# Attention outputs moved to a bank of the feed-forward pool, and first-layer matrices converted 1024 columns at a time

## The chip, the cores and the metric

One core of one Trainium2 chip runs the whole program. The metric is the device time of one execution in microseconds (us); lower is better. Engines: PE (TensorE matmul), DVE (VectorE), ACT (ScalarE), POOL (GpSimd), SP (the queue that issues all DMAs here). PSUM, the accumulator memory that PE writes, has eight banks of 512 float32 columns on 128 partitions.

## The reference

Top-k attention, then two feed-forward blocks, in float32 (weights arrive as float64):

```python
# q, k, v: (4 batches, 8 heads, 576, 64)
scores = scale * q @ k.T
kth = np.partition(scores, -32, axis=-1)[..., -32:-31]     # the 32nd largest of a row
scores = np.where(scores >= kth, scores, -1e9)
attn = softmax(scores); x = attn @ v                       # -> (2304 tokens, 512)
h = x @ w_in;  y = np.maximum(0.01 * h, h) @ w_out         # 512 -> 2048 -> 512
h = np.maximum(np.maximum(y @ w1, y @ w2), y @ w3)         # 512 -> 768, three products
out = h @ moe2_w_out                                       # 768 -> 512
```

## The kernel before, in words

**Attention.** The 2304 tokens are cut into 20 blocks (128 tokens, or 64 at the end of a batch). A *step* handles two heads of a 128-token block or four heads of a 64-token block: 72 steps, 18 for each batch, numbered 0 to 71 in the order of `steps`; the last six make the last 192 tokens. In `attention(i)` PE makes the scores of a head (line 718) into the tile `s`, ACT copies them to SBUF as `S` (L723), DVE finds the 32 largest by four rounds of MAX8 and three of MATCH_REPLACE8 (L738, L740), ACT exponentiates (L788), DVE and POOL mask (L793, L797, L800), ACT and POOL split the result into two float16 parts (L802, L804), one DMA transposes them into `pt` (L807), PE multiplies with v (L833 to L835) into the tile `av`, whose 65th column per head is the row's sum. DVE reads those sums and inverts them (L840, L842), ACT scales the outputs into `xs` (L844), and `xhl` is transposed by DMA into `xu` (L870), the input of the feed-forward part.

**Feed-forward.** `ffn(u)` handles ten units of 192, 128, seven times 256, and 192 tokens. A matmul in float32 accuracy is three float16 matmuls (`three`, L876 to L878). A unit has 16 first-layer tiles of 4 such triples (`h_tile`, drained by ACT at L924), 16 x 4 second-layer triples into the accumulators `acc` (`y_acc`, drained at L974), then 18 x 4 triples of the second block's three products (`m_tile`; ACT drains the first product at L1017, DVE takes the maximum with the other two at L1021) and 6 x 4 output triples (`o_acc`, drained at L1049). Units 0 to 4 need all steps up to 5, 9, 17, 25 and 33; unit 9 needs step 71.

**Weights.** `prep_w` converts the float64 matrices with three DVE operations of integers per piece of `CW` = 512 columns (L499, L502, L505), by way of a PSUM tile: kinds "i" and "o" (w_in and w_out, eight chunks of 1024 columns for either) through one of the two `acc` banks per piece, kinds "t" and "z" (the second block) through a bank of the `h` pool.

**PSUM.** Eight banks: two for one tensor `sav`, in which the scores `s` take columns 0 to 287 of each bank and the attention outputs `av` columns 288 to 417; two `acc` tiles; a pool `h` of four. The pool is shared by the first-layer tiles (at most 2 at a time, `hH`), the tiles of the second block (3, `hM`), conversion pieces (1, `hW`) and small sums over partitions (no limit of their own). The framework that places semaphores serialises accesses of different engines to one bank of one tensor, so whatever touches `s` and whatever touches `av` wait for each other.

**Order.** `Plan.run` is a list scheduler in the program's builder: with estimated durations, latencies and buffer counts (`NB`) it fixes the order of instructions on each engine. Of an engine's ready instructions the one that can start first goes next, and among equals the one of smaller priority number (L139 to L156). An engine then runs its list in that order and waits where something isn't ready. The planner treats `s` and `av` as independent buffers. `RLAG` is an extra delay that it adds before the read of the sums (L840):

```python
279    sav = ps.tile([P, 2, 512], F32, name="sav")
280    ZONE["s"] = [sav[:, :, :288]]
281    ZONE["av"] = [sav[:, :, 288:418]]
...
465    CW = 512
...
680    RLAG = 3.0
```

Of the kernel before, what the change touches and what calls it, by code (L numbers as in the profile page):

```python
# [9 lines left out]
F32 = mybir.dt.float32  # L10
# [19 lines left out]
P = 128  # L30
# [176 lines left out]
def dve(n, fast=False):  # L207
    return (n / (2 if fast else 1) / 0.96 + 69) / 1000
# [6 lines left out]
def dma(nbytes):  # L215
    return nbytes / 255e3
# [3 lines left out]
def attention_moe_kernel(ctx, tc, qk, v, w_in, w_out, w123, w2o, outT):  # L220
# [8 lines left out]

    NB = {"xu": 2, "raw": 2, "hl": 1, "k2": 7, "kt": 4, "qt": 2, "vt": 4, "S": 3, "w": 1, "m": 2, "nb": 2, "pp": 1,  # L230
          "phl": 1, "pt": 1, "r": 2, "xs": 1, "xhl": 1, "f16t": 4, "yj": 1,
          "s": 1, "av": 1, "acc": 2, "h": 4, "junk": 1, "xcap": 2, "pr": 8, "ph": 4, "ra": 3, "fi": 6, "ft": 9, "rw": 3, "fz": 3, "rc": 2, "hH": 2, "hM": 3, "hW": 1, "kH": 2, "kM": 5, "fH": 2, "fM": 2}
    PSUM_TAGS = ("s", "av", "acc", "h")
    plan = Plan(NB, {"raw", "av", "junk", "hl", "k2", "h", "f16t", "rc"})
    op = plan.op
# [2 lines left out]
    def buf(tag, shape, dt=F32):  # L238
        pl = ps if tag in PSUM_TAGS else sb

        def make():
            cnt[0] += 1
            if tag in ZONE:
                return ZONE[tag].pop(0)
            return pl.tile(shape, dt, tag=tag, bufs=NB[tag], name=f"{tag}_{cnt[0]}")

        b = plan.buf(tag, make)
        if tag in ZONE:
            b.done = lambda: ZONE[tag].append(b.ap)
        return b  # L250

    def fbuf(tag, ph, shape, dt=F32):
        b = buf(tag, shape, dt)
        b.also = (plan.buf({"h": "h", "k2": "k", "f16t": "f"}[tag] + ph, lambda: 1),)
        return b
# [20 lines left out]
            "ph": [wof[:, 11264 + 1152 * i:12416 + 1152 * i].rearrange("p (a s) -> p a s", a=2) for i in range(4)],  # L276
            "fz": [w2f[:, 1536 * e:1536 * e + 1536].bitcast(I32) for e in range(1, 4)]}
    NCOL = 318
    sav = ps.tile([P, 2, 512], F32, name="sav")
    ZONE["s"] = [sav[:, :, :288]]  # L280
    ZONE["av"] = [sav[:, :, 288:418]]
    colt = cp.tile([P, NCOL], F32, name="colt")
    cpos = [0]

# [176 lines left out]

    SC = {}
    ZT = "xu"
    CVK = "iotz"
    CW = 512
    CVX = 0.0
    PRW0 = -13.5
    GATES = {1: [], 2: [("d", 0, 0, 0, 1)]}

    def prep_w(kind, c, parts, hi, lo, colnorm, n2c, s, bi, pr, tags, guard=((), (), []), gate=()):  # L470
# [8 lines left out]
        for i, saps in enumerate(parts):  # L479
            nf = sum(n for _, n in saps)  # L480
            f = buf(tags[1], [P, 768 if tags[1] in ("raw", "xu") else 512], I32)
            o = 0
            for sap, n in saps:
                raw = buf(tags[0], [P, 768])
                op(SP, 0.55, lambda raw=raw, sap=sap, n=n: Y.dma_start(raw().bitcast(I64)[:, :n], sap),
                   w=([(f, "ld")] if tags[1] in ("raw", "xu", "k2") or tags[0] in ("raw", "xu") else []) + [raw, (key, "ld")],
                   r=list(gate) + zr + (zf + [("l1", hp, a) for hp in range(HP) for a in range(2)] * (kind == "z" and ZT == "raw") + guard[2] * (tags[1] in ("raw", "xu")) if kind in "tz" else []), pr=PRW0 if (kind, c) == ("i", 0) else pr,
                   dma=dma(P * n * 8))
                for q in range(0, n, CW):
                    cw = min(CW, n - q)  # L490
                    w = lambda raw=raw, q=q, cw=cw: raw().bitcast(I32)[:, 2 * q:2 * (q + cw)].rearrange("p (n t) -> p n t", t=2)
                    t = lambda f=f, cw=cw, q=q + o: f()[:, q:q + cw]
                    pb = None
                    if kind in CVK:
                        pb = buf("acc", [P, 2, UN]) if kind in "io" else fbuf("h", "W", [P, 512])
                    m = t if pb is None else (lambda pb=pb, cw=cw, two=kind in "io": (
                        pb().rearrange("p a n -> p (a n)") if two else pb()).bitcast(I32)[:, :cw])
                    mk_ = [(f, o)] if pb is None else [pb]
                    op(DVE, dve(cw, pb is None) + CVX * (pb is not None), lambda w=w, m=m: V.tensor_scalar(  # L499
                        m(), w()[:, :, 1], 3, 0x3FFFFFFF, op0=ALU.logical_shift_left, op1=ALU.bitwise_and),  # L500
                       r=[raw] + zr + zf, w=mk_, pr=pr)
                    op(DVE, dve(cw) + CVX * (pb is not None), lambda w=w, m=m: V.scalar_tensor_tensor(  # L502
                        m(), w()[:, :, 0], 29, m(), op0=ALU.logical_shift_right, op1=ALU.bitwise_or),
                       r=[raw] + zr + zf, w=mk_, pr=pr)
                    op(DVE, dve(cw) + CVX * (pb is not None), lambda w=w, t=t, m=m: V.scalar_tensor_tensor(  # L505
                        t(), w()[:, :, 1], -0x40000000, m(), op0=ALU.bitwise_and, op1=ALU.bitwise_or),
                       r=[raw] + zr + zf + mk_ * (pb is not None), w=[(f, o)], pr=pr)
                for q in range(0, n, 512):
                    m = min(n - q, 512)
                    sq.append(((f, o), lambda f=f, q=q + o, m=m: f()[:, q:q + m].bitcast(F32), m))  # L510
                o += n
            fs.append((f, [(f, x) for x in np.cumsum([0] + [n for _, n in saps[:-1]]).tolist()],
                       lambda f=f, n=nf: f()[:, :n].bitcast(F32), nf))
# [68 lines left out]
    def w1_prep(f, pr):  # L582
        prep_w("t", f, [[(w123[f, j], 512)] for j in range(3)],
               [w1[:, f, 0, j] for j in range(3)], [w1[:, f, 1, j] for j in range(3)],
               (P, lambda i, kk: (i, kk == 0, kk == 3)), c1(ct, f), c1(s_t, f), c1(bt, f), pr,
               ("rw", "ft" if 1 <= f < 4 else "k2"),
               (["ZA", "ZB"] if f == 0 else [], ["ZR"] if f == 0 else [("ZF", f - 2)] if f >= 3 else [],
                ["ZR"] if f < 3 else [("ZF", f - 2)]), gate=GATES[2])

    def w2_prep(e, pr):  # L590
        for hp in range(HP) if ZT == "raw" else ():
# [85 lines left out]
        return TE + TS * i if i < NE else TA0 + TA * i  # L677

    EXPP = 4
    RLAG = 3.0  # L680
    COLD = 1.7
    NCOLD = 8
    FM = 1
# [12 lines left out]
    def attention(i):  # L696
# [115 lines left out]
            XHL[blk] = buf("xhl", [P, 2, HP, P], F16)  # L812
        xhl = XHL[blk]
        xs = buf("xs", [P, 4, 64])
        avb = buf("av", [P, 512])
        av = lambda: avb().rearrange("p x (h e) -> p x h e", e=65)
        avh = lambda a: av()[:, a // 2, a % 2] if not full else av()[:, 0, a]
        for j in range(2):
            vt = VT[b, hps[j]]

            def avm(j=j, vt=vt):
                hs = [(j, slice(0, P), j)] if full else [(hh, slice(64 * hh, 64 * hh + 64), 2 * j + hh)
                                                        for hh in range(2)]
                for hh, qs, a in hs:
                    o = avh(a)[:qs.stop - qs.start, :]
                    for c in range(5):
                        if c < 4:
                            ch, k = c + 5 * j, 2 * c + hh
                        else:
# [7 lines left out]
            op(PE, 15 * mm(64) * (1 if full else 2) * (COLD if i < NCOLD else 1), avm, r=[pt] + [(vt, x) for x in range(3)], w=[avb, (xs, "a"), (xhl, "a", i)], pr=pa)  # L837
        nh = 2 if full else 4
        r = buf("r", [P, 8])
        op(DVE, 0.07, lambda: V.tensor_scalar(r()[:n, 0:nh].rearrange("p (x h) -> p x h", h=2),  # L840
                                             av()[:n, 0:nh // 2, :, 64], 1e-9 * PS, None, op0=ALU.add), r=[avb], w=[(r, 0)], pr=pr, lag=RLAG)
        op(DVE, 0.08, lambda: V.reciprocal(r()[:n, 4:4 + nh], r()[:n, 0:nh]), r=[(r, 0)], w=[(r, 1)], pr=pr)  # L842
        for h in range(nh):
            op(ACT, act(64, True, 1), lambda h=h: A.activation(xs()[:n, h], avh(h)[:n, 0:64], AF.Copy,  # L844
# [35 lines left out]
    def accs(n):  # L880

        if n <= P:
            a = [buf("acc", [P, 4, P])] * 4
            return (lambda e: a[e]()[:, e, :n]), (lambda e: (a[e], e)), (lambda e: (a[e], "st")), (0,)
        a = [buf("acc", [P, 2, UN]) for _ in range(2)]
        return ((lambda e: a[e // 2]()[:, e % 2, :n]), (lambda e: (a[e // 2], e)), (lambda e: (a[e // 2], "st")),
                (0, 2))

    MAXP = 40
# [304 lines left out]
```

## Time and profile before

| | |
|---|---|
| median of 3 runs | 1131.72 us (1130.45 to 1133.53) |
| the profiled execution's own time | 1129.44 us |
| its span, first to last instruction | 1127.3 us |
| mean granted TensorE clock | 0.958 of full |
| busy: PE / DVE / ACT / POOL | 917.1 / 972.9 / 757.2 / 687.1 us (81 / 86 / 67 / 61%) |

The span is what the trace covers; the time outside it is 2.1 us. A busy share is an average over stretches with different limits: DVE has little to do before the first scores and after the last step, PE has little before the weights are ready. A line such as `L840` is the line of the kernel that issued the instruction; `r<-sav` reads "writes r, reads sav".

### The profile page before, as it was taken

How to read it: one execution, taken by the hardware profiler on the slowest of the kernel's cores; microseconds unless marked ns; L12 is line 12 of the kernel's file. 1: busy time of each engine (PE TensorE's matmuls, PEld its weight loads, DVE VectorE, ACT ScalarE, POOL GpSimd, SP SyncE). 2: the span in 40 equal slices, each digit the busy share in tenths (PEclk: the TensorE clock that was granted, in tenths of full speed). 3: DMA queues.
4: the chain of work that ended last, by engine and by line, in shares of the span. 5: the costliest groups of instructions: out<-in, count | busy, mean ns of one | idle time of the engine just before them, and what ended most of it. 6: DMA issues, size and time to landing. Idle time of an engine off the chain costs nothing.

```text
span 1127.3 us, 27415 instructions
## 1 busy us (share of the span) xinstructions
PE 917.1 (81%) x10292; PEld 800.9 (71%) x10292; DVE 972.9 (86%) x2154; ACT 757.2 (67%) x1625; POOL 687.1 (61%) x1054
## 2 busy tenths in 40 slices
PE   2253236764798998998879899989999998999998
PEld 1132235753698887987768788878888887888998
DVE  3999999999899999999999899899999999995101
ACT  7578757987468666568778665685886665665342
POOL 5475657776458655568678555675887566466121
PEclk9999996875799999999999999999999999999999
DMA  8748457667334432335664423363663433432000
GB/s 297 232 120 258 150 148 211 161 177 150 81 77 103 83 87 52 82 69 143 165 164 97 82 64 72 62 157 75 153 155 77 103 62 53 79 66 53 24 1 16
DMA packets 268517, 125.79 MB, mean 112 GB/s; under 512 B 237408, under 2 KB 255328, under 8 KB 266336
## 3 DMA queue, kind: packets, MB, share of 16 engines
q1 hardware_dynamic: 268384, 124.04, 45.1%
q8 instruction: 81, 1.33, 0.5%
q14 instruction: 52, 0.43, 0.1%
HBM read 62.65 MB, written 14.16 MB: 68 GB/s over the span
## 4 chain that ended last, share of the span: by engine, by line
PE 47%; DVE 16%; ACT 11%; DMA 10%; POOL 7%; issue 6%; SPq 1%; POOLq 0%; ACTq 0%; DVEq 0%
PE h L876 8%; PE h L877 8%; PE h L878 8%; DMA pt<-phl 6%; PE acc L877 5%; PE acc L876 5%; PE acc L878 5%; PE sav L718 4%; DVE m L738 4%; DVE w L740 3%; ACT S L723 2%; PE sav L833 2%; PE sav L834 2%; PE sav L835 2%; DVE w L505 2%
## 5 line engine op out<-in xcount | busy, mean ns | idle before, releaser
L738 DVE MAX8 m<-w 128x8 f32<-128x576 f32 x432 | 309.8, 746 | 0.2 <-DVE r L840 0.2
L937 POOL TENSOR_TENSOR f16t<-k,f16t 128x256 f16<-128x256 f32 (+2 forms) x220 | 144.4, 658 | 175.5 <-ACT f16t L931 150.2
L804 POOL TENSOR_TENSOR phl<-pp,phl 128x576 f16<-128x576 f32 x144 | 184.1, 1288 | 50.5 <-ACT phl L802 49.8
L740 DVE MATCH_REPLACE8 w<-m,w 128x576 f32<-128x576 f32 x288 | 212.0, 741 | 0.0
L876 PE MATMUL h<-k,w 128*128 128x256 f16 (+2 forms) x720 | 187.2, 264 | 7.3 <-ACT k L977 4.0
L877 PE MATMUL h<-k,w 128*128 128x256 f16 (+2 forms) x720 | 187.0, 264 | 3.4 <-POOL k L979 3.3
L878 PE MATMUL h<-k,w 128*128 128x256 f16 (+2 forms) x720 | 186.9, 264 | 0.0
L877 PE MATMUL acc<-f16t,wo 128*128 128x256 f16 (+2 forms) x640 | 167.0, 265 | 5.3 <-POOL f16t L937 5.0
L876 PE MATMUL acc<-f16t,wo 128*128 128x256 f16 (+2 forms) x640 | 166.9, 265 | 0.9 <-ACT k L974 0.5
L878 PE MATMUL acc<-f16t,wo 128*128 128x256 f16 (+2 forms) x640 | 166.9, 265 | 0.0
L718 PE MATMUL sav<-kt,qt 128*128 128x288 f16 (+5 forms) x800 | 109.7, 288 | 61.9 <-ACT S L723 45.9
L876 PE MATMUL h<-xu,wi 128*128 128x256 f16 (+1 forms) x576 | 154.9, 269 | 6.1 <-DMA xu<-xhl 5.3
L877 PE MATMUL h<-xu,wi 128*128 128x256 f16 (+1 forms) x576 | 154.9, 269 | 0.0
L878 PE MATMUL h<-xu,wi 128*128 128x256 f16 (+1 forms) x576 | 154.9, 269 | 0.0
L802 ACT ACTIVATE phl<-pp 128x576 f16<-128x576 f32 x144 | 96.8, 679 | 54.4 <-DVE pp L793 22.7
L788 ACT ACTIVATE pp<-S,nb,colt 128x576 f32<-128x576 f32 x144 | 121.2, 860 | 16.9 <-POOL phl L804 9.3
L718 PEld LDWEIGHTS <-qt 128*128 128x128 f16 (+1 forms) x800 | 64.7, 109 | 87.3 <-issue 71.7
L931 ACT ACTIVATE f16t<-k 128x256 f16<-128x256 f32 (+2 forms) x220 | 85.7, 392 | 52.3 <-DVE k L1021 49.6
L800 POOL TENSOR_TENSOR pp<-pp,S 128x576 f32<-128x576 f32 x72 | 92.1, 1279 | 43.4 <-DVE S L797 32.7
L833 PE MATMUL sav<-vt,pt 128*128 128x65 f16 (+1 forms) x800 | 92.7, 203 | 29.3 <-DMA pt<-phl 22.8
L924 ACT ACTIVATE k<-h,colt 128x256 f32<-128x256 f32 (+2 forms) x160 | 71.0, 451 | 64.1 <-PE h L878 63.8
L723 ACT ACTIVATE S<-sav 128x576 f32<-128x576 f32 x144 | 92.4, 642 | 29.6 <-PE sav L718 14.5
(136 smaller groups left out, 2643.3 us busy)
## 6 DMA issues: line engine op xcount, KB each, us to landing
w<-in_w SPq DMA_DIRECT2D x18, 512.0 KB, 3.9
w<-in_w_in SPq DMA_DIRECT2D x8, 1024.0 KB, 7.2
w<-in_w_out SPq DMA_DIRECT2D x8, 1024.0 KB, 5.0
raw<-in_qk SPq DMA_DIRECT2D x24, 288.0 KB, 3.4
dqk<-hl SPq DMA_DIRECT2D x48, 144.0 KB, 2.5
kt<-dqk SPq DMA_DIRECT2D x16, 288.0 KB, 3.3
qt<-dqk SPq DMA_DIRECT2D x144, 32.0 KB, 2.2
raw<-in_v SPq DMA_DIRECT2D x12, 352.0 KB, 3.4
```

The source lines that it names most:

```text
L718: T.matmul(p()[osl, h, o:o + w], q()[:, hh, st, :n], k()[:, hh, kc:kc + w], start=st == 0, stop=st == 1, skip_group_check=True)
L723: op(ACT, act(S, True), lambda t=t, p=p: A.activation(t().rearrange("p (a s) -> p a s", a=2), p()[:, :, :288], AF.Copy), r=[p], w=[(Sp, j) ...
L738: op(DVE, dve(S) * 1.03, lambda mc=mc, src=src: V.max(mc(), src()), r=rd, w=[(m, j, 0, r)], pr=pd)
L740: op(DVE, dve(S) * 1.03 + 0.06, lambda mc=mc, src=src, j=j: V.match_replace(out=wj(j), in_to_replace=mc(), in_values=src(), imm_value=NEG) ...
L788: op(ACT, act(S, aps=2), lambda j=j, es=es: A.activation(pp()[:, j], Sb[j](), AF.Exp, bias=nb()[:, j:j + 1], scale=es[:, 0:1]), r=[(Sp, j) ...
L802: op(ACT, act(S), lambda j=j: A.activation(phl()[:, 0, j], pp()[:, j], AF.Copy), r=[(pp, j)], w=[(phl, 0, j)], pr=pr)
L804: op(POOL, pool(S), lambda j=j: G.tensor_tensor(phl()[:, 1, j], pp()[:, j], phl()[:, 0, j], op=ALU.subtract), r=[(pp, j), (phl, 0, j)], w= ...
L833: T.matmul(o, hc, vh, start=c == 0, stop=False, skip_group_check=True)
L876: T.matmul(out, wt(0), xt(0), start=first, stop=False, skip_group_check=True)
L877: T.matmul(out, wt(0), xt(1), start=False, stop=False, skip_group_check=True)
L878: T.matmul(out, wt(1), xt(0), start=False, stop=last, skip_group_check=True)
L937: op(POOL, pool(N) + 0.044, lambda: G.tensor_tensor(hl()[:, 1, :N], g()[:, 0, :N], hl()[:, 0, :N], op=ALU.subtract), r=[(g, 0), (hl, 0)], ...
```

## The change

The attention outputs of a step go to a bank of the `h` pool, at most one at a time (`hA`), and all heads of a step lie in that one bank; the scores `s` keep two banks as a tensor of their own. The two `acc` banks become one tensor `acct`, so that kinds "i" and "o" are converted 1024 columns at a time through both banks. Kinds "t" and "z" keep 512. `RLAG` becomes 2.0. The loads of the second block's first matrices (`w1_prep`) are gated on another DMA of batch 0. The constants `CVK`, `CW`, `CVX` go; their values made no difference to the planned durations of the other kinds.

```diff
-          "s": 1, "av": 1, "acc": 2, "h": 4, ... "hH": 2, "hM": 3, "hW": 1, ...
+          "s": 1, "av": 1, "acc": 2, "h": 4, ... "hH": 2, "hM": 3, "hW": 1, "hA": 1, ...
-    sav = ps.tile([P, 2, 512], F32, name="sav")
-    ZONE["s"] = [sav[:, :, :288]]
-    ZONE["av"] = [sav[:, :, 288:418]]
+    acct = ps.tile([P, 2, 512], F32, name="acct")
+    ZONE["acc"] = [acct[:, x] for x in range(2)]
+    accw = acct.rearrange("p a n -> p (a n)").bitcast(I32)
...
+                CW = 1024 if kind in "io" else 512
                 for q in range(0, n, CW):
...
-                    if kind in CVK:
-                        pb = buf("acc", [P, 2, UN]) if kind in "io" else fbuf("h", "W", [P, 512])
+                    if kind in "io":
+                        mk_ = [buf("acc", [P, 512]) for _ in range(2)]
+                        m = lambda cw=cw: accw[:, :cw]
+                    else:
+                        pb = fbuf("h", "W", [P, 512])
+                        mk_ = [pb]
+                        m = lambda pb=pb, cw=cw: pb().bitcast(I32)[:, :cw]
...
-                ["ZR"] if f < 3 else [("ZF", f - 2)]), gate=GATES[2])
+                ["ZR"] if f < 3 else [("ZF", f - 2)]), gate=[("d", 0, 1, 0, 1)])
...
-    RLAG = 3.0
+    RLAG = 2.0
...
-        avb = buf("av", [P, 512])
-        av = lambda: avb().rearrange("p x (h e) -> p x h e", e=65)
-        avh = lambda a: av()[:, a // 2, a % 2] if not full else av()[:, 0, a]
+        avb = fbuf("h", "A", [P, 512])
+        av = lambda: avb()[:, :260].rearrange("p (h e) -> p h e", e=65)
+        avh = lambda a: av()[:, a]
...
-        op(DVE, 0.07, lambda: V.tensor_scalar(r()[:n, 0:nh].rearrange("p (x h) -> p x h", h=2),
-                                             av()[:n, 0:nh // 2, :, 64], 1e-9 * PS, None, op0=ALU.add), r=[avb], w=[(r, 0)], pr=pr, lag=RLAG)
+        op(DVE, 0.07, lambda: V.tensor_scalar(r()[:n, 0:nh], av()[:n, 0:nh, 64], 1e-9 * PS, None, op0=ALU.add), r=[avb], w=[(r, 0)], pr=pr, lag=RLAG)
...
-        a = [buf("acc", [P, 2, UN]) for _ in range(2)]
+        a = [buf("acc", [P, 512]) for _ in range(2)]
```

## Rows read from the trace of the kernel before

**Rows 1.** Busy time by stage: stretch, length, busy of each engine, PEclk, DMA share, GB/s.
```profile
0.00:184.00 184.00, 67.00 (x579) 46.78 (x580) 162.50 (x351) 130.11 (x215) 106.24 (x182) 0.95 0.66 200
184.00:378.00 194.00, 147.62 (x1918) 134.35 (x1917) 182.95 (x414) 143.90 (x330) 131.32 (x212) 0.83 0.56 132
378.00:582.00 204.00, 185.15 (x2023) 160.64 (x2022) 193.12 (x433) 141.75 (x310) 133.92 (x197) 1.00 0.44 104
582.00:1127.00 545.00, 517.28 (x5776) 459.15 (x5775) 434.32 (x959) 341.45 (x771) 315.64 (x466) 0.99 0.36 77
```

**Rows 2.** PE's timeline where unit 4 starts.
```profile
582.24 0.37 PE L876 MATMUL h<-xu,wi 128*128 128x256 f16 x1 [5.34 <-DMA xu<-xhl]
```

**Rows 3.** Waits of DVE over the whole span: us in total, times, longest.
```profile
DVE r L840 <- PE sav L718: 15.0, 14, 2.7
DVE r L840 <- ACT S L723: 7.0, 8, 2.2
DVE r L840 <- PE sav L835: 3.2, 1, 3.2
```

**Rows 4.** The timeline around one late read of the sums: start, us, engine, line.
```profile
639.74 0.19 PE L835 MATMUL sav<-vt,pt 128*128 128x65 f16 x1
...
640.09 0.74 DVE L738 MAX8 m<-w 128x8 f32<-128x576 f32 x1
...
642.72 0.66 PE L718 MATMUL sav<-kt,qt 128*128 128x64 f16 x6
...
643.48 0.16 DVE L840 TENSOR_SCALAR r<-sav 128x2 f32<-128x2 f32 x1 [2.65 <-PE sav L718]
...
645.78 0.31 ACT L844 ACTIVATE xs<-sav,r 128x64 f32<-128x64 f32 x1 [0.74 <-PE sav L718]
```

**Rows 5.** Waits of PE, 582 to 1127 us: us in total, times, longest.
```profile
PE sav L833 <- DMA pt<-phl: 8.0, 8, 2.7
...
PE sav L718 <- ACT S L723: 2.5, 5, 1.5
PE sav L718 <- ACT xs L844: 2.3, 4, 1.4
...
PE sav L833 <- ACT S L723: 1.6, 2, 0.8
...
PE sav L718 <- DVE r L840: 1.0, 1, 1.0
```

**Rows 6.** Waits of DVE, 0 to 378 us.
```profile
DVE r L840 <- PE sav L718: 3.9, 3, 1.7
```

**Rows 7.** Waits of DVE, 378 to 582 us.
```profile
DVE r L840 <- PE sav L718: 4.4, 4, 1.6
...
DVE r L840 <- ACT S L723: 1.5, 1, 1.5
```

**Rows 8.** DVE's timeline inside the conversion of w_out.
```profile
111.29 0.69 DVE L502 SCALAR_TENSOR_TENSOR acc<-w,acc 128x512 int32<-128x512 int32 x1
...
112.01 0.69 DVE L505 SCALAR_TENSOR_TENSOR w<-w,acc 128x512 int32<-128x512 int32 x1
...
121.68 1.27 DVE L499 TENSOR_SCALAR acc<-w 128x512 int32<-128x512 int32 x2
122.87 1.28 DVE L502 SCALAR_TENSOR_TENSOR acc<-w,acc 128x512 int32<-128x512 int32 x2
```

**Rows 9.** Conversion on DVE, groups by shape: count, busy us, mean ns.
```profile
L499 DVE TENSOR_SCALAR h<-w 128x512 int32<-128x512 int32 x18 | 12.2, 678 | 0.6 <-DMA w<-in_w 0.6
L499 DVE TENSOR_SCALAR h<-xu 128x384 int32<-128x384 int32 x8 | 4.4, 554 | 1.9 <-DMA xu<-in_w2o 1.9
```

**Rows 10.** Line 499 for w_in and w_out: duration ns min/median/max, first and last start.
```profile
L499 DVE TENSOR_SCALAR acc<-w x32: 678/682/695, 9.7 to 134.3; 128x512 int32<-128x512 int32 x32
```

**Rows 11.** Issues of line 384, batch 0: ns min/median/max, first and last start.
```profile
L384 SPq DMA_DIRECT2D dqk<-wo x16: 574/592/687, 11.3 to 31.0; - x16
```

**Rows 12.** Issues of line 485, w1 to w3, the same columns.
```profile
L485 SPq DMA_DIRECT2D w<-in_w x18: 327/402/601, 147.7 to 215.5; - x18
```

## What the change does to the time, predicted before it was run

> **What bounds the kernel now.** I read the busy time by stage first, with cuts where unit 0 begins on PE, and units 2 and 4 (184, 378 and 582 us) [rows 1]. Up to 378 us DVE is the full engine: 162.5 of 184 and 183.0 of 194 us, while PE has 67.0 and 147.6. From 378 to 582 us both are nearly full, DVE 193.1 and PE 185.2 of 204 us, and what starts unit 4 is its tokens: PE sat idle 5.34 us for the transposed outputs of step 33 [rows 2]. From 582 us to the end PE has 517.3 of 545 us, 95%, and DVE only 434.3: there the end is set by PE's work, and only a PE wait that goes makes the program shorter. So before 582 us a saving on DVE counts, and after it a saving on PE.
>
> Then the waits of DVE: the read of the sums, L840, waited 15.0 us for score matmuls (L718), 7.0 us for the copy of scores (L723), and only once, 3.2 us, for the matmuls whose result it reads (L835) [rows 3]. The timeline shows one case [rows 4]. The last attention matmul ends at 639.93, DVE is free at 640.83, yet L840 runs at 643.48, behind the next score matmuls, which write the same banks. It cost DVE 2.65 us, and the second read of the outputs (L844 at 645.78) waits for score matmuls again. PE pays too: after 582 us it waited 2.3 us for L844 and 1.0 us for L840 before scores, and 1.6 us for L723 before attention matmuls [rows 5].
>
> **The change, part by part.**
>
> *Scores and outputs in separate banks.* The waits of L840 for L718 and L723 have no reason left, since no bank holds both. Until 378 us they are 3.9 us [rows 6], until 582 us 4.4 + 1.5 = 5.9 us more [rows 7]. After 582 us the rest of them, about 12 us of the 22.0, buys DVE time that PE doesn't follow. There the PE waits count: 2.3 + 1.0 + 1.6 = 4.9 us vanish. The 8.0 us for the transposed probabilities and 2.5 us for S before the second head's scores [rows 5] stand behind DVE and ACT, which run earlier now; bounds 0 and 10.5 us, and I take 3, as POOL and the transposing DMA also stand in that chain and don't become faster.
>
> *RLAG 2.0.* L840 stands about 1 us earlier in DVE's list, and everything behind it there (MAX8 and MATCH_REPLACE8 of the next step) waits if L835 is late. In the one case shown DVE came 0.9 us after L835's end and would have come at about the same moment. With one wait of 72 on L835 now [rows 3], I put it between 0 and 23 waits (as many as L840 has now) of 0.5 us, half of the shift, so 0 to 11.5 us of DVE's time; I take 2 us, 1 in each of the two stretches that DVE paces.
>
> *Conversion in pieces of 1024.* There are 16 chunks of 3 operations, so 48 instructions in place of 96. Two pieces in a row take 1.19 us from start to start (122.87 - 121.68), 0.595 each [rows 8]. A column costs (678 - 554) / 128 = 0.97 ns [rows 9], so that one of 1024 takes 0.595 + 0.496 = 1.09 us: 0.10 us saved in each of 48, 4.8 us. Against it: operations of two pieces alternated, now each depends on the one just before it. A dependent one started 0.72 us after the start of its source (112.01 - 111.29) instead of 0.595 [rows 8], 0.125 us per link. 16 x 2 links within chunks and 15 between make 5.9 us, if DVE has nothing to put in between. It mostly has: the planner takes whatever can start first, and the top-32 search of steps 3 to 5 is pending. So the bounds are a gain of 4.8 and a loss of 1.1 us; I take a gain of 3. All of it lies before 140 us [rows 10], on DVE, where it counts; conversions end later and searches earlier by the same work. The Trainium skill (Perfetto Trace Analysis, "Optimizing Scalar/DVE Operations") gives a DVE operation on PSUM about 125 ns of overhead and advises grouping; by it 48 x 0.125 = 6.0 us would go, an estimate, and the gain in the sum would be 3 us larger. The rows put it lower: the part of 0.595 us that doesn't scale with columns is about 0.10 us, and the page's figure has no links in it.
>
> *Both `acc` banks at once* delay nobody: no unit accumulates before 184 us, and the last of these conversions begins at 134.3 us [rows 10]. *The other gate* costs nothing: the loads are issued from 147.7 us on, the last DMA of batch 0 that it could name was issued at 31.0 us [rows 11, 12]. The change adds and moves no DMA of its own, so SP's and POOL's lists change only through the new plan. That plan may reorder any engine; I put this at zero, with 5 us to either side, the longest PE wait that a late input made in the second half [rows 2].
>
> *One `h` bank for the outputs.* It is held from the first attention matmul until L844 has read it: in the timeline from before 639.74 to 646.09, over 6 us [rows 4]. The limits of the feed-forward tiles (2 and 3) stay, so three tiles and one output fill the pool exactly; PE can now wait for a bank that L844, L1017 or L1021 frees late. The trace has no such wait; the nearest is PE waiting for L844 on the score banks, 4 times, 0.58 us on average [rows 5]. In a unit the second block has 18 x 4 + 6 x 4 = 96 of its 224 triples, 43%, so of the 38 steps after unit 4's start about 16 meet a full pool. At 0.58 us for a third of them that is 3 us, which I take; bounds 0 and, at half of a 6.2 us hold each, 50.
>
> **The sum**, against the profiled execution's 1129.4 us (span 1127.3 and 2.1 around it): until 378 us 3.9 + 3 - 1 = 6; until 582 us 5.9 - 1 = 5, which the 5.34 us idle before unit 4 lets PE use; after it 4.9 + 3 - 3 = 5. Together 16, so 1113.4 us. The median of the runs stands 2.3 us above the profiled one, so I expect a median of 1115.7 us.
>
> **Rivals.**
>
> *PE takes it back.* If the conversion links stay empty (3.9 - 1.1 - 1 = 2 until 378 us), if unit 4 is held by unit 3's own end on PE (1 us of 5 left) and if PE's waits only change their name (0 after 582 us), 3 us remain: 1128.7. For it: PE is 91% busy even from 378 to 582 us. Against it: the 4.9 us are waits on shared banks, and their reason goes. Chance 0.15.
>
> *The full pool: slower.* PE waits for a bank in the second block, because outputs are held over 6 us and PE runs its list in order. The gains beside it are 6 + 5 + 8 = 19 us. With 16 steps after 582 us it decides at 19 / 16 = 1.2 us a step, and shows as slower from 1.4 us, which is the longest wait of PE for L844 now [rows 5]. At 1.9 us a step it costs 30 us: 1131.7 + 11 = 1143. For it: hold times, and PE at 95%. Against it: the planner knows the limit and places outputs and tiles accordingly, as it didn't know of the shared score banks. The Trainium skill (Perfetto Trace Analysis, "Matmuls") says independent matmul groups should rotate through different banks so that draining one overlaps the next; taking one of four from that rotation speaks for this rival. No row before shows PE short of a bank of that pool. Chance 0.17.
>
> *More than forecast.* With 4.8 on conversion, all L840 waits gone at no price of RLAG, and all of the 10.5 us behind DVE, the gain is 8.7 + 5.9 + 15.4 = 30 us: 1101.7. This is the low end of the forecast, not a case of its own.
>
> **How the numbers follow.** The forecast has 0.68. About 0.3%, 3.4 us, is what a measurement of this kernel can tell from no change. Faster 0.68, the same 0.15, slower 0.17. The range goes from 1101 to 1138 us: the low end above, and upward through the first rival into the mild half of the second (1.6 us a step), leaving out about 0.2. The likeliest case alone would be 1101 to 1126.
>
> **What would show it.** Right: L840 waits for L835 alone, some 5 us in all; PE's waits for L844 and L840 before scores are gone; conversion of "i" and "o" in 48 operations of about 1.2 us, with searches between them; unit 2 starts near 372 us, unit 4 near 571, and PE stays over 95% busy behind it. Wrong: PE before `h` tiles or before L833 waiting for L844, L1017 or L1021 for more than 15 us; L840 waiting over 12 us for L835; unit 4 starting no earlier than now; or a new list in which PE idles elsewhere by as much.

## The result, and the profile after

The changed kernel took 1148.11 us (median of 4 runs, 1145.84 to 1153.91); the kernel before, beside it, 1131.18 us (4 runs, 1130.45 to 1133.53). The ratio is 1.0145, interval 1.0121 to 1.017: slower by 17 us, outside the predicted range. The profiled execution took 1145.84 us, with a span of 1144.1 us.

Most lines moved up by one or two: scores L717, copy of scores L722, sums L839, attention matmuls L832 to L834, `three` L874 to L876, drains L922 (first layer), L972 (`y_acc`), L1015 and L1019 (second block), L1047 (outputs), conversion L498, L501, L504.

The busy time by stage, at the same cuts as [rows 1] (the last stretch ends with the span):

```profile
0.00:184.00 184.00, 71.10 (x626) 50.97 (x627) 164.80 (x316) 133.94 (x221) 112.78 (x188) 0.74 0.72 204
184.00:378.00 194.00, 139.99 (x1806) 128.63 (x1804) 183.32 (x414) 144.32 (x328) 127.25 (x209) 0.81 0.53 131
378.00:582.00 204.00, 187.19 (x2110) 163.03 (x2108) 191.79 (x431) 134.75 (x300) 128.73 (x193) 0.99 0.44 94
582.00:1145.00 563.00, 523.02 (x5759) 462.36 (x5757) 428.82 (x950) 346.39 (x778) 315.51 (x465) 0.99 0.36 78
```

After 582 us PE issues about the same number of matmuls as before (5759 and 5776) and the stretch is 18 us longer; DVE has less to do than before. So the time is lost on PE's side, in the stretch where PE sets the end. The clock is hardly a part of it: 0.99 there in both. (Before 184 us it was 0.74 in place of 0.95; a kernel of group 2 below has 0.75 there and loses nothing.)

Waits of PE, changed kernel, whole span (us in total, times, longest):

```profile
PE h L832 <- DMA pt<-phl: 37.1, 24, 5.1
...
PE acct L874 <- ACT k L1047: 7.8, 15, 0.8
PE h L874 <- ACT k L1015: 7.0, 3, 3.1
PE h L874 <- ACT k L975: 5.7, 6, 1.2
PE acct L874 <- ACT k L972: 5.4, 10, 0.6
PE h L875 <- POOL k L977: 5.1, 11, 0.9
```

And the only wait of DVE before the read of the sums, which answers to [rows 3]:

```profile
DVE r L839 <- PE h L834: 7.1, 8, 4.1
```

The second list is what the prediction wanted: the sums wait for their own matmuls alone, 7.1 us in place of 25.2. The first has two lines that nobody forecast: 25 matmuls into the accumulators wait for a drain (L1047, L972), 13.2 us in all. Before there were 3 such waits, 1.3 us:

```profile
PE acc L876 <- ACT k L1049: 0.8, 2, 0.5
...
PE acc L876 <- ACT k L974: 0.5, 1, 0.5
```

The timeline of PE and ACT in unit 9, where no attention is left, shows one:

```profile
1109.74 0.25 PE L875 MATMUL acct<-f16t,wo 128*128 128x192 f16 x1
1109.82 0.25 PE L876 MATMUL acct<-f16t,wo 128*128 128x192 f16 x1
1110.10 0.42 ACT L972 ACTIVATE k<-acct,colt 128x192 f32<-128x192 f32 x1 [1.60 <-PE acct L876]
1110.58 0.24 PE L874 MATMUL acct<-f16t,wo 128*128 128x192 f16 x1 [0.51 <-ACT k L972]
...
1111.27 0.73 ACT L972 ACTIVATE k<-acct,colt 128x192 f32<-128x192 f32 x2 [0.74 <-PE acct L876]
```

Matmuls follow one another every 0.08 us. Then ACT drains the first of the four quarters of the unit's second-layer output. Quarters one and two lie in one bank, three and four in the other. PE's next accumulation is for the third quarter, in the other bank, and starts only when that drain is over: 0.76 us from one matmul to the next. ACT's next two drains then wait for PE in turn. Such drains stand on the chain of waits that ended last, in the same stretch:

```profile
1077.07 0.48 ACT k L1047
1077.59 0.27 PE acct L874
...
1110.10 0.43 ACT k L972
1110.58 0.24 PE acct L874
```

### The profile page after: what moved, and what is told of

Its sections match the earlier page's. It is cut to its first block, busy times and chain, and to the rows that moved or that the text cites. A ratio compares the mean times of both kernels' runs of the same rounds, so it can differ in the third digit from the quotient of the medians.

```text
span 1144.1 us, 27337 instructions
## 1 busy us (share of the span) xinstructions
PE 921.3 (81%) x10292; PEld 805.0 (70%) x10292; DVE 968.7 (85%) x2106; ACT 759.4 (66%) x1625; POOL 684.3 (60%) x1054
## 4 chain that ended last, share of the span: by engine, by line
PE 46%; DVE 19%; DMA 12%; ACT 11%; issue 6%; POOL 5%; SPq 1%; POOLq 0%; ACTq 0%; DVEq 0%
DMA pt<-phl 8%; PE h L874 7%; PE h L875 7%; PE h L876 7%; DVE m L737 7%; DVE w L739 6%; PE acct L874 5%; PE acct L876 5%; PE acct L875 5%; PE s L717 3%; PE h L832 2%; POOL phl L803 2%; PE h L833 2%; PE h L834 2%; ACT k L972 1%
## 5 line engine op out<-in xcount | busy, mean ns | idle before, releaser
L874 PE MATMUL h<-k,w 128*128 128x256 f16 (+2 forms) x720 | 190.1, 268 | 15.0 <-ACT k L1015 7.0
L875 PE MATMUL h<-k,w 128*128 128x256 f16 (+2 forms) x720 | 190.0, 268 | 5.1 <-POOL k L977 5.1
L876 PE MATMUL h<-k,w 128*128 128x256 f16 (+2 forms) x720 | 190.0, 268 | 0.0
L874 PE MATMUL acct<-f16t,wo 128*128 128x256 f16 (+2 forms) x640 | 167.0, 265 | 6.4 <-ACT k L972 5.4
L875 PE MATMUL acct<-f16t,wo 128*128 128x256 f16 (+2 forms) x640 | 167.0, 264 | 0.9 <-POOL f16t L935 0.8
L876 PE MATMUL acct<-f16t,wo 128*128 128x256 f16 (+2 forms) x640 | 166.9, 264 | 0.0
L874 PE MATMUL h<-xu,wi 128*128 128x256 f16 (+1 forms) x576 | 155.0, 269 | 2.0 <-DVE pp L792 1.7
L876 PE MATMUL h<-xu,wi 128*128 128x256 f16 (+1 forms) x576 | 154.8, 269 | 0.0
L717 PE MATMUL s<-kt,qt 128*128 128x288 f16 (+5 forms) x800 | 111.3, 290 | 47.4 <-ACT S L722 36.9
L832 PE MATMUL h<-vt,pt 128*128 128x65 f16 (+1 forms) x800 | 92.1, 203 | 47.4 <-DMA pt<-phl 37.1
L832 PEld LDWEIGHTS <-pt 128*128 128x128 f16 (+1 forms) x800 | 81.0, 105 | 57.4 <-DMA pt<-phl 56.2
L875 PEld LDWEIGHTS <-w 128*128 128x128 f16 x960 | 95.6, 100 | 35.3 <-issue 26.6
L922 ACT ACTIVATE k<-h,colt 128x256 f32<-128x256 f32 (+2 forms) x160 | 71.9, 452 | 73.1 <-PE h L876 72.5
```

The costliest lines, as they stand in the source:

```text
L717: T.matmul(p()[osl, h, o:o + w], q()[:, hh, st, :n], k()[:, hh, kc:kc + w], start=st == 0, stop=st == 1, skip_group_check=True)
L832: T.matmul(o, hc, vh, start=c == 0, stop=False, skip_group_check=True)
L874: T.matmul(out, wt(0), xt(0), start=first, stop=False, skip_group_check=True)
L875: T.matmul(out, wt(0), xt(1), start=False, stop=False, skip_group_check=True)
L876: T.matmul(out, wt(1), xt(0), start=False, stop=last, skip_group_check=True)
```

## The experiments

Four theories. **A**: as one tensor, the two accumulator banks are serialised between engines, so a drain of one bank holds PE's matmuls into the other (and, with 512 columns, conversion pieces in the two banks hold each other). **B**: the full `h` pool, the prediction's second rival. **C**: conversion 1024 columns at a time moves other work, the second block's matrices above all. **D**: the front is held by the chain of conversions up to the last matrix, for which unit 0's second block and unit 1's first layer wait. Medians of the kernel before were 1130 to 1131 us in all comparisons.

**1. The parts, one at a time.** First the outputs in the `h` pool with RLAG 2.0, the accumulators left as two tensors and the conversion at 512 columns (against the kernel before; `hA` = 1 comes with it):

```diff
-    sav = ps.tile([P, 2, 512], F32, name="sav")
-    ZONE["s"] = [sav[:, :, :288]]
-    ZONE["av"] = [sav[:, :, 288:418]]
...
-    RLAG = 3.0
+    RLAG = 2.0
...
-        avb = buf("av", [P, 512])
+        avb = fbuf("h", "A", [P, 512])
```

> The attention outputs in a bank of the h pool, the scores in a tensor of their own and RLAG 2.0; accumulators as two tiles and conversion in 512 columns, as before. Theory A (the two accumulator banks made one tensor, so that PE's matmuls into one bank wait for ACT's drain of the other, about 12 us): those waits are under 2 us and the time is 1128 to 1136 us. Theory B (outputs in the h pool cost the time, a full pool): 1143 us or more. Theory C (conversion in 1024 columns delays the second block's matrices, which start unit 1): unit 1 starts by 318 us as before, the drain waits remain near 13 us, 1138 to 1145 us.

1130.35 us (10 runs), ratio 0.9993, 0.9978 to 1.0008: neither a loss nor a gain. Theory B falls as the cause. Then the two `acc` tiles made one tensor, and nothing else (against the kernel before):

```diff
+    acct = ps.tile([P, 2, 512], F32, name="acct")
+    ZONE["acc"] = [acct[:, x] for x in range(2)]
```

> The kernel before with the two accumulator banks as one tensor, nothing else: conversion in 512 columns, scores and outputs sharing banks, RLAG 3.0. Theory A: PE waits some 10 to 14 us for the drains of the accumulators where it waited 1.3, and the time is 1139 to 1146 us. Theories B and C: no change, 1128 to 1134 us.

1148.83 us, ratio 1.0168, 1.0128 to 1.0207: this edit alone makes all of the loss. All four engines' lists are those of the kernel before. PE's waits and DVE's timeline in the conversion:

```profile
PE acct L879 <- ACT k L1052: 9.2, 17, 0.8
...
PE acct L879 <- ACT k L977: 3.8, 7, 0.6
```

```profile
125.88 1.42 DVE L502 TENSOR_SCALAR acct<-w 128x512 int32<-128x512 int32 x2
127.34 1.43 DVE L505 SCALAR_TENSOR_TENSOR acct<-w,acct 128x512 int32<-128x512 int32 x2
```

24 waits for drains, 13.0 us. And two conversion pieces in a row now take 1.46 us (127.34 - 125.88) where they took 1.19 [rows 8]: the pieces lie in different banks, but of one tensor. Unit 0 starts at 191.1 us in place of 184.3. Then one tensor and 1024 columns, without the outputs (against the kernel just told of):

```diff
+                CW = 1024 if kind in "io" else 512
...
+                        mk_ = [buf("acc", [P, 512]) for _ in range(2)]
+                        m = lambda cw=cw: accw[:, :cw]
```

> The kernel before with the accumulator banks as one tensor and conversion of w_in and w_out in 1024 columns through both; scores and outputs sharing banks, RLAG 3.0. Theory A: as with the one tensor alone within 4 us. Theory B: 1128 to 1134 us. Theory C: 1136 to 1142 us, with unit 1 starting 3 us or more later than before, and no drain waits over 2 us.

1150.88 us, ratio 1.0173, 1.0137 to 1.021. Unit 0 starts at 185.0 us: with the longer pieces 6.1 of the 6.8 us at the start are taken back, but the total doesn't follow. (The lists of this pair differ.) Last the changed kernel with pieces of 512 and the gate of the kernel before (against the changed kernel):

```diff
+    CW = 512
...
-                CW = 1024 if kind in "io" else 512
...
-                ["ZR"] if f < 3 else [("ZF", f - 2)]), gate=[("d", 0, 1, 0, 1)])
+                ["ZR"] if f < 3 else [("ZF", f - 2)]), gate=GATES[2])
```

> The changed kernel with conversion in 512 columns through one accumulator bank each, the two banks still one tensor. Theory A: as the changed kernel, 1143 to 1150 us, with 10 us or more of drain waits. Theory B: the same time, with those waits small. Theory C: 1136 to 1141 us, unit 1 starting by 318 us.

1146.19 us, ratio 1.0133, 1.0077 to 1.0189: as slow as with 1024. Theory C falls: the piece size changes nothing that can be told in the total, in either pair (the interval here is 0.6% to either side). This kernel has the same list on every engine as the first of this group, and differs from it by the merged tensor alone: 1146.19 - 1130.35 = 15.8 us.

**2. The changed kernel with two tensors.** The decisive one: order, gates and conversion steps of the changed kernel, with the accumulators as two tensors; a conversion step is issued as two instructions of 512 columns (against the changed kernel).

```diff
-    acct = ps.tile([P, 2, 512], F32, name="acct")
-    ZONE["acc"] = [acct[:, x] for x in range(2)]
...
+    acc2 = [ps.tile([P, 512], F32, name=f"acct{x}") for x in range(2)]
+    ZONE["acc"] = list(acc2)
...
+                            for x in range(2):
+                                V.tensor_scalar(accw[x], w()[:, hv(x), 1], 3, 0x3FFFFFFF,
...
```

> The changed kernel with its own planned order, gates and 1024-column conversion steps, but with the accumulator banks as two tensors again: each conversion step is issued as two instructions of 512 columns, one for each tensor, and a drain depends on its own bank alone. Theory A (one tensor for both banks): 1125 to 1137 us, that is 11 to 23 us under the changed kernel, with PE's waits for the drains L972 and L1047 down from 13 us to under 2. Theory B (one h bank for the outputs) and theory C (conversion in 1024 columns moves later work): 1143 us or more, since neither the pool nor the order of the conversion is touched.

1130.40 us (10 runs; before 1131.36), ratio 1.0, 0.9978 to 1.0023. The merged tensor costs 17.7 us in the changed kernel. Its waits of PE after 582 us no longer hold a drain of the accumulators:

```profile
PE h L854 <- DMA pt<-phl: 5.9, 10, 1.0
PE h L896 <- ACT k L997: 5.0, 5, 1.2
PE s L739 <- ACT S L744: 3.5, 4, 1.9
PE h L897 <- POOL k L999: 3.4, 8, 0.5
PE h L896 <- ACT k L1037: 2.4, 1, 2.4
PE acct L897 <- POOL f16t L957: 1.6, 4, 0.5
PE h L854 <- DVE m L759: 0.6, 1, 0.6
PE h L896 <- DVE k L1041: 0.6, 1, 0.6
...
```

At the place in unit 9 shown above, the timeline of this kernel has no pause of PE, and ACT drains three quarters in a row:

```profile
1095.80 0.25 PE L898 MATMUL acct<-f16t,wo 128*128 128x192 f16 x1
...
1095.88 0.25 PE L896 MATMUL acct<-f16t,wo 128*128 128x192 f16 x1
...
1096.30 0.25 PE L898 MATMUL acct<-f16t,wo 128*128 128x192 f16 x1
...
1096.08 1.04 ACT L994 ACTIVATE k<-acct,colt 128x192 f32<-128x192 f32 x3 [1.60 <-PE acct L898]
```

PE's list is the same in both, 10292 matmuls one for one, so their starts can be subtracted. From unit 0's start on, the changed kernel falls 17.3 us behind at just 25 of them, all of line 874 into the accumulators, about 0.7 us each. The whole span differs by 1144.1 - 1126.9 = 17.2 us. (Unit 0 starts 4.5 us earlier in the changed kernel; that lead is lost again, bit by bit, at other matmuls.) The memory is the same eight banks: so it is the dependency that the framework draws for a tensor, and not the chip, that makes PE wait.

**3. The pauses taken away in another way.** Each drain is made to depend on all four quarters, so that none stands between PE's matmuls (against the changed kernel):

```diff
-               r=[ak(e), ("ys", u)], w=[(ff, e)], pr=pr)
+               r=[ak(x) for x in range(4)] + [("ys", u)], w=[(ff, e)], pr=pr)
...
-                   r=[ok(e), ("fin", u, b)], w=[(oo, e, b)], pr=pr)
+                   r=[ok(x) for x in range(4)] + [("fin", u, b)], w=[(oo, e, b)], pr=pr)
```

> The changed kernel in which every drain of the accumulators depends on the matmuls into all four quarters, so that ACT begins to drain after PE's last matmul and no matmul into the second bank can wait for the drain of the first. Theory A (merged accumulators): PE's waits for the drains fall from 13.2 to under 3 us, and the time to 1134 to 1141 us. Theory B (the full pool): nothing changes, 1145 to 1150 us.

1123.18 us, ratio 0.993, 0.9904 to 0.9956: 25 us less than the changed kernel, with one wait of 0.7 us for L1047 left. As the planner also finds another order, the 25 us aren't all the pauses. The same edit in the kernel before, and in the kernel before with one tensor, price the rule itself:

> The kernel before with the drains of the accumulators held until all four quarters are accumulated, nothing else. Theory A (the late drain helps only because it takes away waits between the banks of the merged tensor): there are 1.3 us of such waits to take, 1127 to 1136 us. Rival (a late drain is a gain of its own): 1118 to 1125 us.

1134.67 us, ratio 1.0042, 1.0024 to 1.0061: some 5 us lost (2.7 to 6.9) where there was no pause to win.

> The kernel before with the two accumulator banks as one tensor and the drains held until all four quarters are accumulated; conversion in 512 columns, scores and outputs sharing banks. Theory A: PE's waits for the drains fall from 13.0 to under 3 us and the time from 1148.8 to between 1128 and 1139 us; what is left over the kernel before is the conversion, whose pairs took 1.46 us in the one tensor against 1.19. If the waits between the banks are not the cost: 1144 us or more.

1144.09 us, ratio 1.0124, 1.0097 to 1.0152: it won only 4.7 us against the merged tensor alone. The waits for drains are gone there too (L1052: 0.8 us, once). What stays is the conversion at 512 columns with its links in one tensor, and the rule's own 4.8 us (0.42%). Unit 0 starts at 190.3 us, 6.0 us later than before, and against the kernel just told of, which has the same lists, the whole span is 6.2 us longer (1144.1 and 1137.9). 1130.1 + 6.0 + 4.8 = 1140.9, 3 us under what was measured; the rule's price is known to 2 us only, and no run says more of the rest. So the merged tensor does two things, pauses and slower conversion, and pieces of 1024 columns avoid the smaller one, without a gain in the total.

**4. The front.** Theory D: the rule that holds unit 0's second block and unit 1's first layer for the last matrix, taken out of the kernel before, and of the first kernel of group 1.

```diff
-            wk = wkeys("i", [c]) + wkeys("o", range(8)) * (u == 0) + wkeys("z", range(G1)) * (u == 1)
+            wk = wkeys("i", [c]) + wkeys("o", range(8)) * (u == 0)
...
-            wk = wkeys("t", [f]) + (wkeys("t", range(NF2)) + wkeys("z", range(4))) * (u == 0)
+            wk = wkeys("t", [f]) + wkeys("t", range(NF2)) * (u == 0)
```

> The kernel before without the rule that unit 0's second block and unit 1's first layer wait for the last matrix (kind z); the output layer of unit 0 still waits for it. Theory D (the front is held by the chain of conversions up to the last matrix, not by attention): unit 0's second block begins before 285 us where it began at 295, unit 2 begins up to 9 us earlier than 378, and the time is 1121 to 1128 us. Rival (attention on DVE sets the pace up to unit 4): unit 2 begins within 2 us of 378 and the time is 1129 to 1134 us.

1138.53 us, ratio 1.007, 1.0044 to 1.0096. Unit 1 starts at 287.2 in place of 318.5 us, but unit 2 at 377.5 in place of 378.3, unit 4 at 584.3 in place of 582.2, and the rest of the program got longer. The last tokens of unit 2, the outputs of step 17, came at 371.8 us, later than before (368.9), and PE sat idle 3.3 us for them: with shared banks unit 2 waits for its tokens as soon as PE is free. As a way to a faster kernel this missed.

> The outputs alone in the h pool with RLAG 2.0, accumulators and conversion as before, and the same rule on the last matrix taken away. Theory D: with the front no longer held by conversions, the waits of DVE that separate banks removed count up to unit 4, 1113 to 1124 us. Rival: as without the rule and with shared banks, within 3 us.

1118.82 us, ratio 0.9883, 0.984 to 0.9926. With the outputs in the pool alone, the tokens of unit 2 had landed at 374.8 us and PE was what held it until 381.7; without the rule it starts at 376.4 us. But unit 4 starts at 583.5 us, later than with the outputs alone (581.1): nothing of that lead is left. The whole gain lies behind unit 4, 529.2 us to the last matmul in place of 543.5, where the rule holds nothing. So the time fell into the range that theory D had named, but the trace doesn't show theory D as its cause; what differs there is the list. This is the fastest kernel of the study, 29 us under the changed one.

**5. RLAG and the planned order.** The outputs-alone kernel at other values, the kernel before at the same ones, and the late drain at 3.0; each differs from its base by this one line alone (from 2.0 to 3.0 and 2.5 in the first two, from 3.0 to 2.5 and 2.0 in the next two, from 2.0 to 3.0 in the last):

```diff
-    RLAG = 2.0
+    RLAG = 2.5
```

> The outputs alone in the h pool, accumulators and conversion as before, with RLAG 3.0 in place of 2.0. If the 1 us earlier read of the sums took back what separate banks gave (L840 waited 9.8 us for its own matmuls): those waits fall under 4 us and the time to 1120 to 1127 us. If the end is set by PE and by the conversions ahead of unit 0's second block, and DVE's time doesn't count: 1128 to 1133 us.

> The outputs alone in the h pool with RLAG 2.5. If the time follows RLAG: between 1124.1 us (3.0) and 1130.4 us (2.0), 1125 to 1129. If a small change of the planner's inputs moves the time by some us either way: outside of 1123 to 1132 us.

> The kernel before with RLAG 2.5 in place of 3.0, nothing else. If the 1120 us of the outputs-alone kernel at 2.5 come from the separate banks, this one stays at 1128 to 1134 us. If they come from an order that the planner happens to find at 2.5, this one falls to 1123 us or less.

> The kernel before with RLAG 2.0, nothing else. If the separate banks bring 7 to 11 us at equal RLAG, this one is at 1137 us or more (the outputs-alone kernel at 2.0 took 1130). If the banks bring nothing and only the order counts, it is within 4 us of 1130.

> The changed kernel with late drains and RLAG 3.0. If the 1 us earlier read of the sums costs what it seemed to cost with the outputs alone (1130.4 against 1124.1 us): 1115 to 1120 us. If that difference was one of the order that the planner happened to find: 1121 to 1128 us or more.

```
RLAG                             2.0                       2.5                       3.0
scores and outputs share banks   1129.18                   1130.04                   1131.36
  ratio                          0.9985 [0.9966, 1.0005]   0.9982 [0.9963, 1.0]      1
outputs in the h pool            1130.35                   1120.11                   1124.11
  ratio                          0.9993 [0.9978, 1.0008]   0.9913 [0.9882, 0.9945]   0.9934 [0.9907, 0.996]
changed, late drain              1123.18                   -                         1128.62
  ratio                          0.993  [0.9904, 0.9956]   -                         0.9993 [0.9982, 1.0003]
```

With shared banks RLAG does nothing that can be measured. The separate banks give 7 and 10 us at 3.0 and 2.5, and nothing at 2.0, the value that the change took; with late drains it is 2.0 that is better, by some 6 us. The wait for L835's counterpart doesn't explain this: it was 9.8, 6.0 and 4.8 us at 2.0, 2.5 and 3.0. What does differ is the list that the planner makes, and a list is worth up to 10 us; why one is better isn't settled. With separate banks the difference lies behind unit 4, which starts at 581 to 582 us at all three values: from there to the last matmul it is 543.5, 528.6 and 538.6 us. One trait goes with it: in 2-us windows from 576 to 1110 us, the fastest two (1118.82 and 1120.11 us) have no stretch at a granted clock of 0.5, and the kernel before has three, of some 3.4 us each, the first right behind PE's 5.34 us of idling before unit 4 [rows 2]. From unit 4's start on, the kernel at 2.5:

```profile
580.90:1113.00 532.10, 510.08 (x5730) 456.13 (x5729) 426.40 (x948) 339.93 (x770) 310.98 (x461) 1.00 0.36 80
```

and in the kernel before:

```profile
582.00:584.00 2.00, 1.76 (x22) 1.29 (x22) 2.00 (x6) 0.88 (x2) 1.09 (x1) 0.50 0.28 57
```

510.1 us of PE's time for 5730 matmuls, against 517.3 for 5776 in the last stretch of [rows 1]. Part of the 7 us is these matmuls, which come earlier in the other list; how much of the rest is the clock isn't shown. The last kernel put both good edits together, the outputs in the pool at RLAG 2.5 and no rule for the last matrix (the edit of group 4 on the outputs-alone kernel at 2.5):

> Outputs in the h pool alone, RLAG 2.5, accumulators as two tensors, conversion of 512 columns, and without the rule that holds unit 0's second block and unit 1's first layer for the last matrix. If what the outputs bring and what the rule costs add up as they did at RLAG 2.0 (11.5 us), 1108 to 1114 us; if they work at the same stretch of the program, 1115 to 1121 us.

1123.67 us, ratio 0.9935, 0.9914 to 0.9957: faster than both kernels compared here, but outside both expected ranges; the two gains don't add. Here unit 4 does start earlier, at 574.7 in place of 580.9 us, but from there to the last matmul it takes 543.7 in place of 528.6 us, again behind the rule's reach.

## Why the prediction was wrong

**The step that failed** is "*Both `acc` banks at once* delay nobody". I asked only whether a unit's accumulation could meet a conversion in time, found 184 against 134.3 us [rows 10], and stopped. The edit that lets one instruction span two banks is a new tensor, and it holds for the whole program: a drain of one bank orders PE's matmuls into the other. The description of the kernel before says that the framework serialises accesses to "one bank of one tensor"; the runs show that accesses to two banks of one tensor are serialised too: of the accumulators, the tensor decides and not the bank. [Rows 3, 4] can't tell the two readings apart, since scores and outputs shared the banks as well as the tensor; so the price of the new tensor should have been bounded from both sides like the other unknowns, and its upper bound is a drain's wait for each accumulation of each unit. In place of 0 it was 17.7 us (13.2 us in the view of waits; the starts fall back by 17.3, since matmuls overlap: the view counts idle time from the end of the last one, 0.17 us after the next would have started). The Trainium skill (Perfetto Trace Analysis, "Matmuls") says that independent groups should rotate through different banks so that draining one overlaps the next group; here the groups did rotate, and the drain held PE all the same, until the banks were two tensors.

**What bounds the kernel** was read rightly for the time after 582 us, and it is why the mistake was dear: each pause of PE moves the end there. Of the 17.3 us, 11.7 come after unit 4's start, at 17 matmuls. Before 582 us the reading failed as well, as the next terms show.

**The other terms**, from the kernel with two tensors, whose total is the kernel before's within 3 us rather than 16 us below it: the wrong sign comes from the merged tensor, but without it the forecast gain wasn't there either. The starts of units on PE, in us:

```
                               before   forecast   changed   two tensors   outputs alone
unit 2 starts                  378.3    372        384.0     384.6         381.7
unit 2 to unit 4               204.0    199        201.2     197.9         199.4
unit 4 to the last matmul      541.0    536        554.8     540.3         543.5
```

- *Until 378 us* (6 us): the attention did run ahead as the step said, the outputs of step 17 at 361.7 in place of 368.9 us, 7.2 us. But unit 2 doesn't start by that alone. PE was still in unit 1 until 386.1 us (before: 380.4), as unit 1 waits for the last matrix, whose last conversion began at 287.4 in place of 282.9 us: DVE's list put searches first (the outputs of step 9 came at 250.6 in place of 267.6 us). The term fails at "before 582 us a saving on DVE counts"; the likeliest case didn't ask for unit 2 what the first rival asked for unit 4, whether PE is free. Group 4 bears it out for this start: with the rule gone unit 2 starts 5.3 us earlier.
- *378 to 582 us* (5 us): the stretch is shorter by 6.1 and 4.6 us in the two kernels without the merged tensor, but by luck: unit 2 starts 6.4 and 3.4 us later, and unit 4 starts at 582.5 and 581.1 us, where it started at 582.2. With two tensors the outputs of step 33 came at 563.5 in place of 572.8 us, and the 5.34 us of idling are gone. But PE comes without a wait from unit 3's last output triples:

```profile
582.03 0.27 PE L898 MATMUL acct<-f16t,w 128*128 128x256 f16 x1
582.14 0.51 PE L315 MATMUL h<-colt,ones 128*128 128x1 f32 x4
582.51 0.27 PE L896 MATMUL h<-xu,wi 128*128 128x256 f16 x1
```

  This is the first rival's second condition, unit 4 held by unit 3's own end on PE.
- *After 582 us* (5 us): PE's waits for L844 and L840 are gone, as forecast, 4.9 us. With two tensors those behind DVE and ACT (the transposed probabilities and S) went from 10.5 to 9.4 us, so 1 us and not 3. Its waits for a bank of the `h` pool, behind L1015 and L1019 in the new kernel, are 4.0 us (3.0 with two tensors, 4.1 with the outputs alone), so the price of 3 is about right, but half of it or more is a single wait of 2 to 3 us, not small ones at a third of the steps. The prediction says that the trace before has no such wait; it has three over the whole span, one of them, 0.3 us, after 582:

```profile
PE h L876 <- ACT k L1017: 3.2, 3, 1.6
```

  What the sum put at nothing are PE's waits for the second block's inputs, the drained second-layer outputs as float16 parts. Before, after 582 us:

```profile
PE h L876 <- ACT k L977: 2.9, 3, 1.6
...
PE h L877 <- POOL k L979: 1.5, 3, 0.6
```

  These 4.4 us became 7.8 in the changed kernel (L975, L977) and 8.4 with two tensors (L997 and L999 above). So with two tensors -4.9 - 1.1 + 2.7 + 4.0 gives 0.7 us more, where 0.7 us less was measured: PE's waits changed their place, the first rival's third condition, and the second rival's pool stayed far under the 15 us set for it.
- *RLAG* (2 us): with shared banks it is worth nothing that can be told; with separate ones, it changes the list by up to 10 us. The margin of 5 us for a new plan was too small.
- *Conversion* (3 us): mechanism and order as forecast, as DVE's timeline of the changed kernel shows:

```profile
123.56 1.22 DVE L498 TENSOR_SCALAR acct<-w 128x1024 int32<-128x1024 int32 x1
124.69 0.75 DVE L737 MAX8 m<-w 128x8 f32<-128x576 f32 x1
125.36 1.21 DVE L501 SCALAR_TENSOR_TENSOR acct<-w,acct 128x1024 int32<-128x1024 int32 x1
126.48 0.75 DVE L737 MAX8 m<-w 128x8 f32<-128x576 f32 x1
127.15 1.20 DVE L504 SCALAR_TENSOR_TENSOR w<-w,acct 128x1024 int32<-128x1024 int32 x1
```

48 operations, some with searches in between. From the start of one to the next operation it is 1.12 to 1.13 us here; two pieces took 1.19, so 0.06 to 0.07 us are saved in each, 3 us in all. The bound had 0.10 us for each and 4.8 in all; the 3 taken, a choice between two bounds, came out by luck; the 125 ns of the Trainium skill (Perfetto Trace Analysis, "Optimizing Scalar/DVE Operations") would be twice what the rows show. Unit 0 did start earlier, 178.8 against 183.3 us with two tensors. Apart from the pauses 3.0 us of this are left at unit 4 and 0.1 at the end, so in the total it was worth nothing.

**The rivals.** The first, at 1128.7 us, is what the change comes to without the merged tensor (1130.4), by two of its three conditions; it had a chance of 0.15. The second had the right sign and a close time (1143) with the wrong cause: outputs alone lose nothing. The mechanism that decided, the drains holding PE, stood in none of them. The chance of slower, 0.17, was therefore put on a case that didn't occur.

## What to carry to other kernels

Before two buffers become one tensor, list who writes and who reads each of them over the whole program, not only in the edit's own stage: what the builder orders by tensor, it orders for every later use. Here an edit worth 3 us in conversion, and nothing in the total, cost 17.7 us in accumulation; issuing a step as two instructions on two tensors avoids it. When a kernel's order comes from a planner, compare pairs that keep the list (the same instructions on each engine) to price a cause, and expect up to some 10 us from a new list by itself. Say of a gain in which stretch it lies before giving it a cause.

## What of the hardware wasn't expected

- A pause of PE costs more than the drain it waits for: the drain lasts 0.42 us, the step from matmul to matmul is 0.76 in place of 0.08 us, since the drain begins 0.28 us after the last matmul's start and the next matmul starts 0.06 us after its end.
- The short pauses hardly move the clock: with 17 of them after unit 4's start the changed kernel has four stretches at a granted clock of 0.5 from 576 us until its last matmul, the kernel before three, each some 3.4 us long. The fourth begins at about 1113 us, behind the pause shown above and two waits of 1.07 and 0.44 us for the second block's inputs. (0.5 is the lower of the two levels, 1.2 of 2.4 GHz.) Behind 5.34 us of idling before unit 4 [rows 2] it fell to that level.
- The chip itself shows no objection to ACT draining one bank while PE accumulates into another: with two tensors they overlap in the timeline (matmuls into the second bank from 1095.88 to 1096.30, the drain from 1096.08 us), as the Trainium skill says of different banks (PSUM — Partial Sum Buffer, "PSUM bank collisions raise a hardware error").
